# A block-sparse attention with two gated layers on one core: the second batch's value means, two iterations later

## The chip, the cores and the metric

The kernel runs on one core of one Trainium2 chip. The metric is the device time of one execution in microseconds (us). The core has five engines that take their instructions in order, each from its own stream: TensorE (PE in the profile, with its weight loads as PEld), VectorE (DVE), ScalarE (ACT), GpSimd (POOL) and SyncE (SP), which here only issues transfers.

## The reference

Three stages, all in float32. The attention has 2 batches, 8 heads, 768 positions and 64 values per head. Each query sees the keys within 15 positions of its own and, for the whole sequence, 24 block entries: the maximum of the keys and the mean of the values over blocks of 32.

```python
k_sum = k.reshape(B, H, nb, block, D).max(axis=3)
v_sum = v.reshape(B, H, nb, block, D).mean(axis=3)
scores_l = scale * np.matmul(q, k.transpose(0, 1, 3, 2))
mask_l = np.abs(pos[:, None] - pos[None, :]) < window
scores_s = scale * np.einsum('bhsd,bhnd->bhsn', q, k_sum) + np.log(block)
scores_all = np.concatenate([np.where(mask_l, scores_l, -1e9), scores_s], axis=-1)
a = softmax(scores_all)                  # written out, with 1e-09 on the sum
out = np.matmul(a, np.concatenate([v, v_sum], axis=2))
...
h = x @ w_in;  g = h / (1 + exp(-1.702 * h));  x = g @ w_out            # 512 -> 2048 -> 512
...
x = (sigmoid(x @ w_gate) * (x @ w_val)) @ w_out2                        # 512 -> 1536 -> 512
```

The 2 x 768 rows of the attention, with the 8 heads side by side, are the 1536 rows of the two gated layers.

## The kernel before

**Units.** The attention is cut into 24 units: 2 batches, 3 groups of 256 queries, 4 pairs of heads. Units 0 to 11 are the first batch, 12 to 23 the second. A unit's scores are 4 tiles of 128 x 128: 64 queries of two heads against 32 columns for the block entries and 96 for a window of keys. The loop runs over t from -1 to 26, and each iteration t issues the steps of several units, as `ORDER` (L789) says: `w_copy` (POOL, keys and block maxima of unit t+1 to the tile `kx`), `b_pe` (PE, scores `ps_s` of unit t), `b_max` (DVE, L715), `b_exp` (ACT, L723), `n_inv` and `n_mul` (DVE and POOL, unit t-1), and for unit t-3 `c_pe` (PE, transposes `ps_p`, L743), `c_copy` (L748, on ACT up to unit 9, on DVE from unit 10), `d_pe` (PE, products with the values, `ps_x`, L762), `d_hi` (ACT, L780) and `d_lo` (DVE, L783).

**Means of the values.** `sum_load` (L657) brings the transposed values of one pair of heads to a tile `vt`, of which there are two buffers, so the third load waits for the first sum and the fourth for the second. `sum_v` (L668) sums them over blocks of 32 on DVE (L672, into `vm`). `sum_lay` (L677) transposes the four pieces on PE (`ps_v`, L681, with an identity) and scales them on ACT into `vs` (L682). `put_v` (L648) copies `vs` to the first 32 rows of four places of the tile `vwin`, by a transfer; `load_v` (L640) brings the windows of the values to its other 96 rows (L646). `vwin` holds two groups of 256 queries in turn. The second batch's first group is read by `d_pe` of unit 12, in iteration 15. `ps_v` and `ps_x` share one PSUM tag, "x", with two buffers.

**Keys.** `load_k` (L624) brings the second batch's keys in iterations 8 to 11, one pair of heads in each; `prep_k` (L684) takes their block maxima on DVE (L688) at the start of iterations 10 to 13.

**Other work of the same stretch.** The first weights of the gated layers are loaded (`fetch`, L229) and split into two parts by `load` (L118; DVE L132, L150, L157, ACT L140, L155), called through `pull`. From iteration 10 on `filler` (L843) issues products of the first gated layer (`ps_h`, `ps_o`, L489; gate on ACT L522, DVE L500, ACT L508, POOL L509), so that PE has work beside the attention. After the attention PE does the gated layers.

**Order.** SP's transfers are issued in the order in which the program writes them, apart from a few weight pieces, and a transfer that waits holds those behind it. On PE, DVE, ACT and POOL a planner orders the instructions when the program is built: it takes what it expects to be ready, earlier program lines first, by its own costs. On the chip each engine keeps to that order. SP's order around the change, from iteration 7 on, is in each iteration: the query block of unit t+5, a transposed value (t = 7 to 10), the window values and `put_v` (t = 7, 11, 15, 19), the keys (t = 8 to 11), and weight pieces.

Of the kernel before, what the change touches and what calls it, by code (L numbers as in the profile page):

```python
# [29 lines left out]
def attention_moe_moe2_kernel(ctx: ExitStack, tc: tile.TileContext, ins: dict, out: bass.AP):  # L30
# [15 lines left out]
    NG = NQB // G  # L46
# [182 lines left out]
    def fetch():  # L229

        if pieces:
            name, src = pieces.pop(0)
            n, m = src.shape[1], src.shape[2]

            home, tag = (xp, "xH") if name == "1_0_1" else (wraw, "raw")
            raw = home.tile([P, n * m], U32, tag=tag, name=f"{tag}{name}")
            nc.sync.dma_start(out=raw.rearrange("p (a n) -> p a n", a=n), in_=src)
            raws.append((raw, (P, n, m // 2)))
# [355 lines left out]
    def pull(n):  # L594
        for _ in range(n):
            next(coming, None)
# [9 lines left out]
    with tc.manual_schedule(engines={mybir.EngineType.SP}), ExitStack() as es:  # L606
# [17 lines left out]
        def load_k(b, hp):  # L624

            t = kp.tile([P, SH], F32, tag="k", name=f"k{b}_{hp}")
            nc.sync.dma_start(out=t, in_=k[b, hp])
            kraw[b, hp] = t

        def load_q(u, eng):  # L630

            b, g, hp = units[u]
            t = qp.tile([P, G, P], F32, tag="q", name=f"q{u}")
            eng.dma_start(out=t.rearrange("p i c -> p (i c)"), in_=q[b, g, hp])
            qbd[u] = t
# [4 lines left out]
        def load_v(b, g):  # L640
            c = (b * NG + g) % 2 * G
            first_row = v[b, g * G * QB:g * G * QB + P - W0, :]
            src = bass.AP(
                first_row.tensor, first_row.offset, [first_row.ap[0], [QB * H * D, G], [1, H * D]]
            )
            nc.sync.dma_start(out=vwin[W0:P, c:c + G, :], in_=src)  # L646

        def put_v(b, g, eng=nc.sync):  # L648
            c = (b * NG + g) % 2 * G
            src = vsum[b][0:W0].unsqueeze(1).to_broadcast([W0, G, H * D])  # L650
            eng.dma_start(out=vwin[0:W0, c:c + G, :], in_=src)
# [5 lines left out]
        def sum_load(b, hp):  # L657
            if (b, hp) == (0, 2):
                early = xp.tile([P, 2, KC * TB // 2], F32, tag="xL", name="vt_early")
                vtl["early"] = [early[:, i, 0:S] for i in range(2)]  # L660
            if b == 0 and hp > 1:
                t = vtl["early"][hp - 2]
            else:
                t = vp.tile([P, S], F32, tag="vt", bufs=2, name=f"vt{b}_{hp}")
            nc.sync.dma_start(out=t, in_=vt[b, hp])
            vtl[b, hp] = t

        def sum_v(b, hp):  # L668
            if hp == 0:
                vpart[b] = vp.tile([P, HP, W0], F32, tag="vm", name=f"vm{b}")  # L670
                nc.vector.memset(vpart[b], 0.0)
            nc.vector.tensor_reduce(  # L672
                out=vpart[b][:, hp, 0:NB], in_=vtl.pop((b, hp)).rearrange("p (n t) -> p n t", t=BLK),
                axis=AX.X, op=ALU.add,
            )

        def sum_lay(b):  # L677
            r = vpart.pop(b)
            ps = ps_a.tile([W0, H * D], F32, tag="x", name="ps_v", bufs=2)
            for hp in range(HP):  # L680
                nc.tensor.matmul(ps[:, hp * P:(hp + 1) * P], lhsT=r[:, hp], rhs=ident, start=True, stop=True)  # L681
            nc.scalar.activation(vsum[b][0:W0], ps, AF.Copy, scale=1.0 / BLK)  # L682

        def prep_k(b, hp):  # L684
            ks = kp.tile([P, W0], F32, tag="ks", name=f"ks{b}_{hp}")
            nc.vector.memset(ks, 0.0)
            own = kraw[b, hp][:, HALO:HALO + S].rearrange("p (n t) -> p n t", t=BLK)
            nc.vector.tensor_reduce(out=ks[:, 0:NB], in_=own, axis=AX.X, op=ALU.max)  # L688
            kmax[b, hp] = ks
# [164 lines left out]
        for t in range(-1, NU + LD):  # L854
            now[0] = t

            u = t + 2
            if u < NU and units[u][1] == 0:
                prep_k(units[u][0], units[u][2])
            for part, lag in ORDER:  # L860
                if 0 <= t - lag < NU:
                    part(t - lag)
            if 0 <= t < NU - 5:
                load_q(t + 5, nc.sync)
            if t == -1:
                sum_v(0, 0)
                sum_v(0, 1)
            if t == 0:
                sum_v(0, 2)
                sum_v(0, 3)  # L870
                sum_lay(0)
                load_v(0, 1)
                put_v(0, 1, nc.scalar)
            if t in (2, 5, 8):
                fetch()
            if t in (7, 8, 9, 10):
                sum_load(1, t - 7)
            if t in (8, 9, 10, 11):
                sum_v(1, t - 8)
            if t == 11:  # L880
                sum_lay(1)

            if t % HP == HP - 1 and HP < t < NU - HP:
                c = t // HP + 1
                load_v(c // NG, c % NG)
                put_v(c // NG, c % NG)
            if 8 <= t < 8 + HP:
                load_k(1, t - 8)
            if t >= 1:
                pull(1 if t < 6 or t > 9 else 2)  # L890
            for _ in range(2 if t >= 8 else 1):
                next(fill, None)
# [168 lines left out]
```

## Time and profile before

| | us |
|---|---|
| median of 3 runs | 617.34 |
| lowest and highest run | 616.87, 618.29 |
| the profiled execution | 616.23 |
| its span in the profile | 614.4 |
| PE busy | 601.0 |
| DVE busy | 448.6 |
| ACT busy | 313.3 |
| POOL busy | 201.6 |

A group of the profile names a line of the kernel, an engine, an operation, and the tiles out<-in. Idle time of an engine counts only where it lies on the chain that ends last. A busy PE is not PE at its peak, since products are pipelined and their recorded spans overlap.

### The profile page before, as it was taken

The numbers are of one execution on the slowest core, as the hardware profiler recorded it, in microseconds if no ns is written. First come the engines' busy times: TensorE is split into PE (matmuls) and PEld (weight loads), VectorE is DVE, ScalarE is ACT, GpSimd is POOL, SyncE is SP. The second block draws the span as 40 slices with busy tenths as digits, with TensorE's granted clock in tenths as the row PEclk, the third lists the DMA queues.
The fourth block names the chain that finished last, engine by engine and source line by source line (L and its number), as shares of the span: only waits on it lengthen the run. The fifth ranks groups of instructions, "written<-read, shape, count | busy, mean of one in ns | idle before, by whom it ended". The sixth has DMA issues, their size and how long they took to land.

```text
span 614.4 us, 8772 instructions
## 1 busy us (share of the span) xinstructions
PE 601.0 (98%) x3348; PEld 500.4 (81%) x3348; DVE 448.6 (73%) x655; ACT 313.3 (51%) x620; POOL 201.6 (33%) x164
## 2 busy tenths in 40 slices
PE   7888999999999999999999999999999999999997
PEld 4766787788888888888888888898898898898896
DVE  6699665399929988877559889668759669777434
ACT  4678657566424645535345667635445246344230
POOL 6897685323331243413322021022022022122030
PEclk9899999999999999999999999999999999999999
DMA  9998753012402421321002023222222222200014
GB/s 314 343 313 298 233 138 70 2 69 69 137 1 68 138 68 69 103 104 65 5 1 69 0 69 103 104 69 69 69 69 69 68 69 70 68 2 1 0 51 155
DMA packets 25162, 58.10 MB, mean 95 GB/s; under 512 B 1569, under 2 KB 1825, under 8 KB 25121
## 3 DMA queue, kind: packets, MB, share of 16 engines
q1 hardware_dynamic: 24400, 56.24, 28.3%
q10 hardware_dynamic: 720, 1.31, 0.6%
q8 instruction: 26, 0.43, 0.3%
q14 instruction: 16, 0.12, 0.1%
HBM read 53.08 MB, written 3.15 MB: 92 GB/s over the span
## 4 chain that ended last, share of the span: by engine, by line
PE 92%; DVE 3%; POOL 1%; issue 1%; DMA 1%; ACT 1%; SPq 0%; ACTq 0%; POOLq 0%; DVEq 0%
PE ps_o L489 37%; PE ps_y L197 16%; PE ps_x L197 10%; PE ps_v L197 10%; PE ps_h L489 8%; PE ps_h L197 4%; PE ps_s L710 3%; PE ps_x L762 2%; PE ps_p L743 1%; DMA vt<-in_vt 1%; POOL kx L699 1%; DVE nm L715 1%; ACT e L723 1%; DVE da L150 1%; DVE vm L672 0%
## 5 line engine op out<-in xcount | busy, mean ns | idle before, releaser
L509 POOL TENSOR_TENSOR gl<-sg,gh 128x512 fp32r<-128x512 f32 x84 | 125.6, 1500 | 377.3 <-ACT gh L508 290.1
L575 DVE TENSOR_TENSOR acc<-ps_o,acc 128x512 f32<-128x512 f32 x143 | 96.5, 685 | 66.5 <-PE ps_o L489 66.3
L489 PE MATMUL ps_o<-gl,w_1H 128*128 128x512 f32 x192 | 75.3, 393 | 0.0
L489 PE MATMUL ps_o<-gh,w_1H 128*128 128x512 f32 x192 | 74.7, 390 | 0.0
L489 PE MATMUL ps_o<-gh,w_1L 128*128 128x512 f32 x192 | 71.9, 396 | 1.8 <-ACT gh L508 1.7
L508 ACT CAST gh<-sg 128x512 fp32r<-128x512 f32 x84 | 51.7, 622 | 31.1 <-DVE sg L500 24.7
L489 PE MATMUL ps_o<-w_2L,gh 128*128 128x512 f32 (+1 forms) x146 | 56.6, 388 | 0.0
L489 PE MATMUL ps_o<-w_2H,gh 128*128 128x512 f32 (+1 forms) x146 | 56.4, 386 | 0.0
L489 PE MATMUL ps_o<-w_2H,gl 128*128 128x512 f32 (+1 forms) x146 | 56.3, 389 | 0.1
L150 DVE SCALAR_TENSOR_TENSOR da<-da,db 128x1024 uint32<-128x1024 uint32 x34 | 47.7, 1404 | 9.7 <-ACT da L140 9.1
L140 ACT ACTIVATE da<-da 128x1024 f32<-128x1024 f32 x34 | 36.1, 1061 | 21.8 <-DVE da L132 21.8
L489 PEld LDWEIGHTS ps_o<-gh,w_1L 128*128 128x128 f32 x192 | 35.9, 188 | 9.6 <-ACT gh L508 2.2
L489 PEld LDWEIGHTS ps_o<-gl,w_1H 128*128 128x128 f32 x192 | 36.1, 188 | 7.3 <-POOL gl L509 0.2
L489 PEld LDWEIGHTS ps_o<-gh,w_1H 128*128 128x128 f32 x192 | 36.1, 188 | 7.3
L723 ACT ACTIVATE e<-ps_s,nm 128x128 f32<-128x128 f32 x96 | 34.2, 376 | 9.1 <-DVE nm L715 6.9
L699 POOL TENSOR_SCALAR kx<-k 128x384 f32<-128x384 f32 x24 | 32.2, 1344 | 15.7 <-PE ps_s L710 7.1
L489 PE MATMUL ps_h<-xH,w_0L 128*128 128x512 f32 x80 | 31.7, 407 | 0.8 <-DVE db L132 0.8
L710 PE MATMUL ps_s<-kx,q 128*128 128x128 f32 x192 | 30.5, 307 | 1.9 <-POOL kx L699 1.8
L489 PEld LDWEIGHTS ps_o<-w_2H,gh 128*128 128x128 f32 x146 | 27.4, 188 | 5.7
L710 PEld LDWEIGHTS ps_s<-kx,q 128*128 128x128 f32 x192 | 27.5, 215 | 5.6 <-POOL kx L699 3.3
L489 PEld LDWEIGHTS ps_o<-w_2L,gh 128*128 128x128 f32 x146 | 27.5, 188 | 5.0
L489 PEld LDWEIGHTS ps_o<-w_2H,gl 128*128 128x128 f32 x146 | 27.4, 188 | 5.2 <-DVE acc L575 0.3
(244 smaller groups left out, 1495.5 us busy)
## 6 DMA issues: line engine op xcount, KB each, us to landing
raw<-in_moe_w_out SPq DMA_DIRECT2D x13, 1024.0 KB, 4.9
raw<-in_moe_w_in SPq DMA_DIRECT2D x8, 1024.0 KB, 7.3
raw<-in_moe_w_gate SPq DMA_DIRECT2D x6, 1024.0 KB, 5.0
raw<-in_moe_w_val SPq DMA_DIRECT2D x6, 1024.0 KB, 5.1
q<-in_q SPq DMA_DIRECT2D x20, 256.0 KB, 8.9
vwin<-in_v SPq DMA_DIRECT2D x6, 768.0 KB, 9.4
k<-in_k SPq DMA_DIRECT2D x8, 400.0 KB, 7.2
out<-acc SPq DMA_DIRECT2D x11, 256.0 KB, 2.0
```

The source lines that it names most:

```text
L140: nc.scalar.activation(af, af, AF.Prelu, scale=REBIAS, alpha=-2.0 ** 32)
L150: ins = nc.vector.scalar_tensor_tensor(out=a, in0=a, scalar=3, in1=b, op0=ALU.logical_shift_left, op1=ALU.bitwise_or)
L197: nc.tensor.matmul(ps, lhsT=a[x][:, kk, :], rhs=b[y][:, kk, :], start=start and i == 0, stop=i == n - 1, skip_group_check=True,)
L489: nc.tensor.matmul(ps, lhsT=a, rhs=b, start=i == 0, stop=i == n - 1)
L508: nc.scalar.copy(gh, sg)
L509: nc.gpsimd.tensor_tensor(out=gl, in0=sg, in1=gh, op=ALU.subtract)
L575: added[layer, g, blk, m] = nc.vector.tensor_tensor(out=a[:, m, :], in0=ps, in1=a[:, m, :], op=ALU.add)
L699: nc.gpsimd.tensor_scalar(out=to, in0=x, scalar1=scale, scalar2=None, op0=ALU.mult)
L710: nc.tensor.matmul(ps[:, j, :], lhsT=t[:, j, :], rhs=kt[:, j, :], start=False, stop=j == G - 1)
L715: nc.vector.tensor_reduce(out=nm, in_=live["s", u], axis=AX.X, op=ALU.max, negate=True)
L723: nc.scalar.activation(e[:, j, :], s[:, j, :], AF.Exp, bias=nm[:, j:j + 1], accum_out=sm[:, j:j + 1])
L762: nc.tensor.matmul(ps[64 * e:64 * e + 64, j, :], lhsT=x[:, h * D:(h + 1) * D], rhs=y[:, j, 64 * e:64 * e + 64], start=n == 0, stop=n == le ...
```

## The change

The loads of the second batch's transposed values move from iterations 7 to 10 to iterations 9 to 12, the sums from 8 to 11 to 10 to 13, and `sum_lay` from 11 to 13. `put_v(1, 0)`, which copies the second batch's means to its first group's places, moves from iteration 11, where it followed `load_v(1, 0)`, to iteration 13 behind `sum_lay`; `load_v(1, 0)` stays in iteration 11. The later groups' `put_v` stay (NG is 3, and c counts the groups over both batches).

```diff
             if t in (2, 5, 8):
                 fetch()
-            if t in (7, 8, 9, 10):
-                sum_load(1, t - 7)
-            if t in (8, 9, 10, 11):
-                sum_v(1, t - 8)
-            if t == 11:
+            if t in (9, 10, 11, 12):
+                sum_load(1, t - 9)
+            if t in (10, 11, 12, 13):
+                sum_v(1, t - 10)
+            if t == 13:
                 sum_lay(1)
+                put_v(1, 0)
 
             if t % HP == HP - 1 and HP < t < NU - HP:
                 c = t // HP + 1
                 load_v(c // NG, c % NG)
-                put_v(c // NG, c % NG)
+                if c != NG:
+                    put_v(c // NG, c % NG)
             if 8 <= t < 8 + HP:
                 load_k(1, t - 8)
```

## Rows read from the trace of the kernel before

**Rows 1.** The page: busy time, share of the span, instructions.

```profile
PE 601.0 (98%) x3348; PEld 500.4 (81%) x3348; DVE 448.6 (73%) x655; ACT 313.3 (51%) x620; POOL 201.6 (33%) x164
```

**Rows 2.** Windows: stretch, its length, busy us by engine, clock, DMA share, GB/s.

```profile
40.00:60.00 20.00, 17.93 (x155) 13.80 (x155) 19.32 (x33) 17.39 (x50) 15.79 (x14) 1.00 0.99 321
60.00:80.00 20.00, 19.29 (x138) 15.49 (x138) 13.14 (x26) 13.76 (x40) 14.54 (x15) 1.00 0.68 220
80.00:100.00 20.00, 20.00 (x170) 16.15 (x169) 12.19 (x28) 11.17 (x43) 13.24 (x16) 1.00 0.51 120
```

**Rows 3.** The chain that ended last, from 46 us: start, us, engine, tile, line.

```profile
46.21 0.69 DVE nm L715
...
57.75 1.56 DVE w_1L L157
...
62.87 0.69 DVE pt L748
...
63.69 0.69 PE ps_x L762 x16
...
69.07 5.46 PE ps_h L489 x24
```

**Rows 4.** Timeline of DVE, 40 to 70 us: start, us, instruction, [idle before <-releaser].

```profile
40.35 0.92 DVE L672 TENSOR_REDUCE vm<-vt 128x24 f32<-128x768 f32 x1
...
48.55 0.95 DVE L672 TENSOR_REDUCE vm<-vt 128x24 f32<-128x768 f32 x1
...
57.08 0.68 DVE L748 COPY pt<-ps_p 128x512 f32<-128x512 f32 x1
...
60.48 0.94 DVE L672 TENSOR_REDUCE vm<-vt 128x24 f32<-128x768 f32 x1
...
68.76 0.95 DVE L688 TENSOR_REDUCE ks<-k 128x24 f32<-128x768 f32 x1 [2.57 <-DMA k<-in_k]
```

**Rows 5.** Timeline of SP, 31 to 64 us: start and us of each issue.

```profile
31.38 0.38 SPq L665 DMA_DIRECT2D vt<-in_vt  x1
...
41.29 0.33 SPq L665 DMA_DIRECT2D vt<-in_vt  x1
...
50.89 0.38 SPq L646 DMA_DIRECT2D vwin<-in_v  x1
62.60 0.61 SPq L651 DMA_DIRECT2D vwin<-vs  x1
63.30 0.54 SPq L627 DMA_DIRECT2D k<-in_k  x1
```

**Rows 6.** Waits of SP (whole span) and of PEld (40 to 80 us).

```profile
SPq L651 <- ACT vs L682: 11.2, 1, 11.2
PEld ps_x L762 <- DVE xL L783: 0.6, 2, 0.4
```

**Rows 7.** Tile vt: durations, landing; transfers of means issued at 62.60 and 32.69.

```profile
L672 DVE TENSOR_REDUCE vm<-vt x6: 917/945/954, 8.0 to 60.5; 128x24 f32<-128x768 f32 x6
...
DMA to landing us min/median/max: 5.9/7.4/12.2
...
vwin<-vs SPq DMA_DIRECT2D x1, 256.0 KB, 3.3
...
vwin<-vs SPq DMA_DIRECT2D x1, 256.0 KB, 11.4
```

**Rows 8.** Timeline of PE, 51 to 75 us.

```profile
51.84 0.62 PE L681 MATMUL ps_v<-ident,vm 128*32 128x128 f32 x4
...
60.92 0.69 PE L762 MATMUL ps_x<-pt,vwin 128*64 128x64 f32 x16
...
74.46 0.45 PE L762 MATMUL ps_x<-pt,vwin 128*64 128x64 f32 x6
```

**Rows 9.** Timeline of POOL: copies of keys at 58 and 79 us.

```profile
58.36 2.22 POOL L699 TENSOR_SCALAR kx<-k 128x384 f32<-128x384 f32 x1
...
79.38 1.17 POOL L699 TENSOR_SCALAR kx<-k 128x384 f32<-128x384 f32 x1
```

## The prediction

> **What bounds the kernel now.** I read the page first: TensorE (PE) is busy 601.0 of 614.4 us [rows 1], so all that PE does not stand idle for is fixed work, and the change alters none of it. The reader should next look where PE does stand idle. The windows answer that: from 40 to 60 us PE is busy 17.93 of 20, from 60 to 80 it is 19.29, and from 80 on it is full [rows 2]. In the same 40 to 60 VectorE (DVE) is busy 19.32 and ScalarE (ACT) 17.39. So the attention stage is set by the vector side, and the rest by PE. The change acts at about 31 to 75 us, on the seam between the two.
>
> The chain of waits says where the seam lies. From 46.21 on it runs through DVE alone (maximum of unit 11, weight splits, block sums), up to the copy of unit 11's transposes at 62.87, which ends at 63.56; at 63.69 it enters PE with unit 11's value products and stays there, with long runs of products such as the 24 at 69.07 [rows 3]. What comes earlier or later at 63.69 comes earlier or later at the end, as PE has a backlog from there on. A loss after it counts only if PE runs dry.
>
> The timeline of DVE shows the first of the four block sums at 40.35, the second at 48.55 and the last at 60.48, each 0.92 to 0.95 long, and at 68.76 the block maximum of the fourth keys after an idle 2.57 that a transfer of keys ended [rows 4]. The timeline of SP shows why that transfer was late: the four transposed values go out from 31.38 on (the third at 41.29), the values of the next window at 50.89, and then the copy of the means waits until 62.60; the keys follow at 63.30 [rows 5]. SP's own waits put 11.2 us on that copy, for ACT's means [rows 6].
>
> **The change, part by part.**
>
> *Loads and sums moved by two iterations.* Four loads, four sums and a memset stay as many; nothing is added. Of the sums the first (40.35) stands before the DVE chain begins, the other three inside it, ahead of the copy at 62.87. After the change the first load goes out where the third does now (about 41), the second about 45, the third beside the row at 50.89, and the fourth about 56, since its buffer waits for the second sum. With 7.4 us to landing, the median of these loads [rows 7], the sums can start at about 48, 53, 58 and 64. The first and second are inside the chain, the fourth is behind it, the third lands at the edge. Three sums inside the chain become two or three. I take two: one sum of 0.95 us leaves the chain. Bounds: 0 (three remain) and 1.9 (only one remains before 62.87, if the sums really move by two whole units). What the sums that leave do next is covered: behind 63.69 DVE has the idle 2.57 at 66 [rows 4], and PE has the runs from 69.07 [rows 3]; without that backlog each would cost its 0.95 there.
>
> *The products that transpose the sums.* These sixteen products share a ring of two PSUM buffers with the value products of the units. Now they take a buffer at 51.84 and hold it until ACT reads the means, just ahead of 62.60; the value products of unit 10 start at 60.92, when the vector engine has emptied the only other buffer [rows 8]. The waits put 0.6 us in two places on that emptying [rows 6]. After the change the buffer is asked for two units later, so units 9 and 10 have both. I credit the recorded 0.6 us. Bounds: 0 (the engine's order holds them anyway) and 3.2, if unit 10 could start right behind the copy of its transposes (57.08 and 0.68 [rows 4]) rather than at 60.92; of this PE had other products to do for much of the time, so I stay by the recorded wait. Holding the buffer later falls under the backlog of PE.
>
> *The transfer of the means.* One transfer of 256 KB with the same 0.6 us of issue on SP, moved from iteration 11 to 13. What stands behind it on SP changes: today the fourth keys, query blocks and two weight pieces stand behind it; afterwards the keys and most of the query blocks go ahead, the weight pieces still stand behind. The keys then go out at about 51 instead of 63.30, and the idle 2.57 of DVE goes. I price this at nothing: PE was covered there by the runs at 69.07. There is a cost: the keys' block maximum (0.95) may now be ready before the copy at 62.87 and be put ahead of it. I take nothing for it and 0.95 as its bound, which would eat the first term. The window's values stay in iteration 11, with no new wait ahead of them.
>
> *The new wait.* Unit 12's value products are the first that read the moved means. They start at 74.46 now [rows 8], and the means have about 9 us of slack, as their transfer took 3.3 us in an empty queue; among other traffic the same transfer took 11.4 [rows 7]. From the start of the last sum to the issue is 2.1 us today (60.48 to 62.60). So in the new order: fourth sum at 64, issue at 66, landing at 69.5 by the quick row and 77.5 by the slow one, against unit 12 at about 73. The queue should be nearly empty by then, since what stood behind has gone ahead, so I take the quick row, and no cost; bound 4.5.
>
> *The sum.* 0.95 + 0.6 = 1.55 us off the profiled execution's 616.23 gives 614.7. That execution lies 1.1 below the median of the runs, 617.34; on the median the forecast is 615.8.
>
> **A rule against it.** The rows show GpSimd's copy of keys taking 2.22 us at 58.36 [rows 9], beside a weight split on DVE at 57.75 that took 1.56 [rows 3], and 1.17 at 79.38; the sums themselves keep to 917 to 954 ns [rows 7]. So a sum may be a pause in which GpSimd runs free, and a chain with fewer sums has its weight splits closer together; two more stretched copies would cost 2 x 1.05 us on the way to the scores. This is rival 3 below. The Trainium skill, SBUF — State Buffer, Who interferes with whom, says that a DVE instruction with two SBUF inputs contends with a GpSimd instruction that reads SBUF, and that a tensor_reduce never does on trn2; by that rule the stretched copies are blocked ones and the sums are harmless, so swapping sums for splits can only hurt GpSimd. The stretched row agrees in direction; no row here shows the lock itself.
>
> **The rivals.**
>
> 1. *Nothing to measure.* Three sums stay inside the chain, or the fourth keys' maximum takes the place of the one that left; only some of the 0.6 remains. For it: the loads land 7 to 12 us after their issue, so a shift by two iterations need not be two units on DVE, and the planner orders DVE by readiness. Against it: the last sum can hardly land before 63. Time: 617.34 less 0 to 0.6, about 617.1.
>
> 2. *The means come too late (slower).* Place: PE at unit 12's value products. It decides if the transfer is issued after 73 - 3.3 = 69.7, or if it lands at the slow row's pace. For it: the moved sums ran about two units behind their own iteration (the sum of iteration 11 stands at unit 13), and the same lag from iteration 13 puts the last one beside unit 15, at the same point as the products that need it; the fourth load can't go out before the second sum; a load took up to 12.2 us [rows 7], which alone puts the issue at 70 or later. Against it: DVE has room after 65, and the DMA queue too. Price: landing at 77.5 instead of 73 is 4.5, less about 0.5 of other units' products and the 1.55 won: 617.34 + 2.5 = 619.8.
>
> 3. *GpSimd loses what DVE wins.* The 2.1 us of two stretched copies against 0.95 won: 618.5.
>
> 4. *DVE stands still for a late load.* DVE executes in order, and a sum placed for 7.4 us to landing that lands after 12.2 holds everything behind it, at worst inside the chain. In the trace all four sums were met without such a wait, against it; that the queue is full there speaks for it. Price: 4.8 us, less 1 to 2 of margin and the 1.55 won: 619.1.
>
> **How the numbers follow.** The forecast has 0.42, rival 1 0.26, rival 2 0.18, rival 3 0.06, rival 4 0.08. A difference of 0.2% is 1.23 us, about what a measurement can tell here. Forecast: faster, 0.42. Rivals 1 and 3 lie within 0.2%: 0.32. Rivals 2 and 4 are slower: 0.26. The range reaches down to 617.34 less the 1.9 of the first bound and half of the 3.2 of the second, 613.8, and up to 619.2, which takes in rivals 1, 3, most of 4 and the light half of 2; some 0.04 lies below and 0.13 above. The likeliest case alone spans 613.8 to 616.1.
>
> **What would show it.** Right: the fourth sum starts after the copy of unit 11's transposes, that copy ends at about 62.6 instead of 63.56, unit 11's value products start near 62, the transposing products start after unit 10's value products, the keys' transfer goes out near 51 with no idle 2.57 behind it, and from there PE is full as before. SP's wait for the means is still there, some 8 us long, in iteration 13. Wrong: a PE wait on the transfer of means ahead of unit 12's value products (rival 2), GpSimd copies of over 2 us in other places (rival 3), a DVE wait on a transposed value between 46 and 64 (rival 4), or unit 11's value products still at 63.7 (rival 1). The whole forecast falls if PE shows new idle time anywhere behind 64, as the planner may order the four engines anew from iteration 7 on.

## The result, and the profile after

The changed kernel took 621.37 us (median of 4 runs, 620.82 to 622.0), the kernel before 617.27 on the same chip (4 runs): a ratio of 1.0074, with a 95% interval of 1.0061 to 1.0086. It is 0.7% slower, where the forecast was 615.8 us and faster; 621.37 lies above the range too. The profiled execution has a span of 619.7 us against 614.4, 5.3 us more, and that is what has to be found.

The page after, as in [rows 1]:

```profile
PE 600.8 (97%) x3348; PEld 499.6 (81%) x3348; DVE 449.0 (72%) x655; ACT 316.0 (51%) x622; POOL 201.2 (32%) x164
```

PE has the same work. ACT has two instructions more and 2.7 us more of work: a pair of table loads of 1.28 each. So PE stands idle longer, or runs at a lower clock. The windows after answer to [rows 2] (same columns), with finer ones behind:

```profile
40.00:60.00 20.00, 16.93 (x157) 13.04 (x158) 18.36 (x34) 17.04 (x50) 13.32 (x13) 0.95 1.04 339
60.00:80.00 20.00, 20.00 (x129) 15.34 (x128) 13.00 (x22) 11.86 (x31) 14.88 (x14) 0.96 0.31 94
80.00:100.00 20.00, 18.71 (x155) 14.99 (x154) 13.37 (x28) 11.00 (x48) 14.14 (x16) 1.00 0.91 249
100.00:120.00 20.00, 17.81 (x150) 14.18 (x150) 8.91 (x23) 16.43 (x48) 8.37 (x8) 1.00 0.00 1
...
55.00:58.00 3.00, 0.79 (x8) 0.62 (x7) 3.00 (x8) 2.97 (x11) 2.20 (x2) 1.00 1.05 253
58.00:60.00 2.00, 1.90 (x19) 1.27 (x19) 2.00 (x6) 2.00 (x5) 0.50 (x2) 0.53 1.06 235
60.00:62.00 2.00, 2.00 (x10) 1.27 (x8) 2.00 (x2) 1.97 (x10) 2.00 (x2) 0.62 1.03 318
62.00:64.00 2.00, 2.00 (x10) 1.41 (x9) 2.00 (x5) 0.00 (x0) 2.00 (x3) 1.00 0.53 196
```

And four windows of the kernel before that are not in [rows 2]:

```profile
55.00:58.00 3.00, 1.31 (x18) 1.13 (x13) 3.00 (x6) 2.98 (x5) 2.74 (x4) 1.00 1.06 258
...
60.00:62.00 2.00, 1.91 (x22) 1.10 (x22) 2.00 (x5) 0.55 (x3) 1.83 (x2) 1.00 0.04 16
62.00:64.00 2.00, 1.39 (x14) 0.89 (x16) 2.00 (x5) 2.00 (x11) 0.53 (x1) 1.00 0.06 15
100.00:120.00 20.00, 19.99 (x166) 15.52 (x166) 9.93 (x24) 14.26 (x48) 9.08 (x10) 1.00 0.01 2
```

Multiply PE's busy time by the granted clock (PEclk, a share of the full 2.4 GHz) and the loss can be placed. The reader is to see three episodes:

- **40 to 64 us.** Before: 17.93 [rows 2] + 1.91 + 1.39 = 21.23 us of work. After: 16.93 less 0.47 x 1.90 for the clock of 0.53, plus 0.62 x 2.00, plus 2.00 = 19.28. Lost: 1.95.
- **80 to 100.** Before full [rows 2]; after 18.71. Lost: 1.29.
- **100 to 120.** 19.99 before, 17.81 after. Lost: 2.18.

Together 5.42, close to the 5.3 of the span. From 64 to 80 both are full. Up to 40 us the same count gives 31.2 before and 30.9 after, so the balance is good to some 0.4 us.

What PE waits for in the three is in its timeline after (start, us, products, idle time and its releaser):

```profile
58.10 0.59 PE L708 MATMUL ps_s<-mask,pick 128*128 128x512 bf16 x1 [2.31 <-ACT e L723]
58.62 1.12 PE L762 MATMUL ps_x<-pt,vwin 128*64 128x64 f32 x16
...
60.44 1.20 PE L489 MATMUL ps_o<-gh,w_1L 128*128 128x512 f32 x2
...
73.05 0.41 PE L681 MATMUL ps_v<-ident,vm 128*32 128x128 f32 x2
...
79.02 0.69 PE L762 MATMUL ps_x<-pt,vwin 128*64 128x64 f32 x16
...
86.66 0.69 PE L762 MATMUL ps_x<-pt,vwin 128*64 128x64 f32 x16 [0.74 <-DVE pt L748]
...
88.70 0.50 PE L489 MATMUL ps_o<-gh,w_1L 128*128 128x512 f32 x1 [0.55 <-DVE acc L575]
...
106.37 0.50 PE L489 MATMUL ps_o<-gh,w_1L 128*128 128x512 f32 x1 [0.58 <-DVE sg L500]
...
112.44 0.69 PE L762 MATMUL ps_x<-pt,vwin 128*64 128x64 f32 x16 [1.62 <-DVE pt L748]
```

*First.* At 58.10 the mask product of unit 15 (it puts the mask into the unit's scores; the other products of those scores come only at 73.38) waits 2.31 us for the PSUM buffer that the exponentials of unit 12 empty, and holds all behind it. ACT's timeline, before and then after, tells why those are late and what else is. A gate batch is two tiles `sg` of the first gated layer that pass the sigmoid together; `gh` is ACT's copy of such a tile, which the products `ps_o` read.

```profile
52.78 1.28 ACT L522 ACT_TABLE_LOAD   x1
...
56.24 0.64 ACT L508 CAST gh<-sg 128x512 fp32r<-128x512 f32 x1
56.90 1.28 ACT L723 ACT_TABLE_LOAD   x1
...
59.58 0.63 ACT L508 CAST gh<-sg 128x512 fp32r<-128x512 f32 x1
```

```profile
52.85 1.28 ACT L522 ACT_TABLE_LOAD   x1
54.15 1.08 ACT L522 ACTIVATE sg<-ps_h 128x512 f32<-128x512 f32 x2
55.25 1.28 ACT L723 ACT_TABLE_LOAD   x1
56.54 0.37 ACT L723 ACTIVATE e<-ps_s,nm 128x128 f32<-128x128 f32 x1
...
59.13 1.16 ACT L508 CAST gh<-sg 128x512 fp32r<-128x512 f32 x2
...
103.70 1.28 ACT L522 ACT_TABLE_LOAD   x1
107.26 1.28 ACT L723 ACT_TABLE_LOAD   x1
```

Before, the gate batch's first copy `gh` comes at 56.24, ahead of the exponentials, and the second at 59.58, behind them; after, the exponentials with their table load come first and both copies at 59.13. So the products `ps_o` that need `gh` start at 60.44. Before, they started at 56.94:

```profile
56.94 0.50 PE L489 MATMUL ps_o<-gh,w_1L 128*128 128x512 f32 x1 [1.69 <-ACT gh L508]
```

And behind the wait PE's clock falls to 0.53 and 0.62 in the profiled execution, that is, it spends most of 58 to 62 us at 1.2 GHz.

*Second.* The chain of waits after runs through the moved means:

```profile
73.20 1.28 ACT L522
74.49 0.60 ACT sg L522
75.09 0.48 ACT vs L682
75.58 0.61 SPq L651
...
76.24 5.75 DMA raw<-in_moe_w_out
...
82.01 1.77 DVE db L132
```

SP issues a weight piece right behind the means, DVE stands 1.75 us idle for it, and PE gets the lateness at 86.66 and 88.70: 0.74 and 0.55 us, together the 1.29.

*Third.* The table loads at 103.70 and 107.26 are the extra pair; ACT is busy 16.43 of 20 us instead of 14.26, and PE waits 0.58 at 106.37 and 1.62 at 112.44, both on the chain of waits that runs through these loads.

DVE's timeline answers to [rows 4]:

```profile
51.19 0.94 DVE L672 TENSOR_REDUCE vm<-vt 128x24 f32<-128x768 f32 x1
...
53.40 0.68 DVE L715 TENSOR_REDUCE nm<-ps_s 128x4 f32<-128x512 f32 x1
...
57.93 0.94 DVE L672 TENSOR_REDUCE vm<-vt 128x24 f32<-128x768 f32 x1
...
62.13 0.68 DVE L748 COPY pt<-ps_p 128x512 f32<-128x512 f32 x1
...
63.06 0.94 DVE L672 TENSOR_REDUCE vm<-vt 128x24 f32<-128x768 f32 x1
...
64.86 0.94 DVE L688 TENSOR_REDUCE ks<-k 128x24 f32<-128x768 f32 x1
...
66.56 0.92 DVE L672 TENSOR_REDUCE vm<-vt 128x24 f32<-128x768 f32 x1
```

### The profile page after: what moved, and what is told of

It is laid out like the page before. It is cut to its first block, busy times and chain, and to the rows that moved or that the text cites. A ratio compares the mean times of both kernels' runs of the same rounds, so it can differ in the third digit from the quotient of the medians.

```text
span 619.7 us, 8778 instructions
## 1 busy us (share of the span) xinstructions
PE 600.8 (97%) x3348; PEld 499.6 (81%) x3348; DVE 449.0 (72%) x655; ACT 316.0 (51%) x622; POOL 201.2 (32%) x164
## 2 busy tenths in 40 slices
DMA packets 25161, 58.10 MB, mean 94 GB/s; under 512 B 1568, under 2 KB 1824, under 8 KB 25120
## 3 DMA queue, kind: packets, MB, share of 16 engines
q1 hardware_dynamic: 24400, 56.24, 28.3%
q10 hardware_dynamic: 720, 1.31, 0.6%
## 4 chain that ended last, share of the span: by engine, by line
PE 85%; DMA 8%; ACT 3%; DVE 3%; issue 0%; SPq 0%; ACTq 0%; DVEq 0%
PE ps_o L489 36%; PE ps_y L197 15%; PE ps_x L197 10%; PE ps_v L197 10%; PE ps_h L489 7%; PE ps_h L197 4%; DMA raw<-in_moe_w_out 3%; DMA xH<-in_moe_w_out 2%; DMA vt_early<-in_vt 2%; PE ps_x L762 1%; DMA q<-in_q 1%; ACT e L723 1%; PE ps_p L743 1%; ACT L723 1%; ACT L522 1%; DVE db L132 1%
## 5 line engine op out<-in xcount | busy, mean ns | idle before, releaser
L132 DVE TENSOR_SCALAR db<-raw 128x1024 uint32<-128x1024 uint32 x33 | 31.6, 959 | 3.6 <-DMA raw<-in_moe_w_out 3.2
L710 PE MATMUL ps_s<-kx,q 128*128 128x128 f32 x192 | 28.6, 296 | 3.8 <-POOL kx L699 2.3
L710 PEld LDWEIGHTS ps_s<-kx,q 128*128 128x128 f32 x192 | 26.0, 206 | 7.6 <-POOL kx L699 3.7
```

What stands on the lines that cost most here:

```text
L132: ins = nc.vector.tensor_scalar(**x)
L710: nc.tensor.matmul(ps[:, j, :], lhsT=t[:, j, :], rhs=kt[:, j, :], start=False, stop=j == G - 1)
```

## The experiments

**Theory 1, the order.** The moved work costs little. The planner, given other due work, writes other orders for PE and ACT, and in a few places these make PE wait. **Theory 2, the moved work itself.** Sums and means are late, and what needs them pays. In the kernels, `behind(a, b)` has the planner place instruction a behind instruction b. It adds no work, but the rest of the plan follows from it, so more than this pair can move. The diffs are shortened: `ins` and `live[...]` name instructions, the lines that store them are left out, and remarks behind # are added. Ratios are to the kernel before on the same chip; the runs come from several chips, so compare ratios rather than times.

| run | median us | ratio, 95% |
|---|---|---|
| after | 621.37 | 1.0074 (1.0061 to 1.0086) |
| e4_mask15 | 621.84 | 1.0079 (1.0059 to 1.0099) |
| e7_lay_first | 621.9 | 1.009 (1.0071 to 1.0109) |
| e2_act_queue | 620.5 | 1.0066 (1.0051 to 1.0081) |
| e5_one_table_pair | 619.12 | 1.0042 (1.0027 to 1.0057) |
| e9_gh_first | 617.05 | 1.001 (1.0 to 1.0021) |
| e13_gh_act | 617.93 | 1.0013 (1.0002 to 1.0024) |
| e3_one_later | 620.03 | 1.005 (1.0033 to 1.0068) |
| e12_one_later_gh | 617.44 | 1.0013 (1.0004 to 1.0022) |
| e1_means_late | 619.4 | 1.0058 (1.0039 to 1.0076) |
| e14_means_late_table | 616.12 | 0.999 (0.9981 to 0.9999) |
| e11_before_exp_first | 619.09 | 1.0045 (1.003 to 1.006) |
| e15_before_gh | 616.9 | 0.9999 (0.999 to 1.0008) |

**e4_mask15: the waiting mask product moved out of the way.** After, with one order more:

```diff
-            nc.tensor.matmul(ps, lhsT=pick, rhs=mask[:, g:g + G, :], start=True, stop=False)
+            ins = nc.tensor.matmul(ps, lhsT=pick, rhs=mask[:, g:g + G, :], start=True, stop=False)
+            u == 15 and behind(ins, live["d10"])     # d10: value products of unit 10
```

> The changed kernel with one order on PE altered: the mask product of unit 15 (one product of 0.4 us, needed only at 73) goes behind the value products and transposes of unit 10 instead of ahead of them; nothing else moves on any engine. In the changed trace PE stands idle 2.31 us ahead of that product at 58.10, and then shows a granted clock of 0.53 and 0.62 up to 62. Theory 1 (order: the loss is made of a few places where a planner's new order makes PE wait): 1.5 to 3 us off the changed kernel's 621.4, about 619. Theory 2 (late means: the loss comes from the transfer of the means at 75.58, which holds SP and pushes unit 12): nothing, 621 to 621.8, as the means come no earlier.

621.84 us: nothing won. PE's timeline shows the wait moved on:

```profile
57.20 0.69 PE L762 MATMUL ps_x<-pt,vwin 128*64 128x64 f32 x16 [1.51 <-DVE pt L748]
...
60.31 1.22 PE L489 MATMUL ps_o<-gh,w_1L 128*128 128x512 f32 x2 [1.35 <-ACT gh L508]
```

Unit 10's value products start earlier (57.20), and then PE stands for `gh`. The mask product was only the first in the line; what PE lacked next was ACT's `gh`.

**e7_lay_first: the means earlier.** After, with the last products that transpose the sums ahead of the second gate batch's products:

```diff
+                (g, blk, f) == (1, 0, 0) and held_up.append(live["lay", 1])
                 held.append(project(w[0], w[1], f, blk, "ps_h"))   # its first product: behind(ins, held_up.pop())
```

> The changed kernel with one order on PE altered: the last transposing product of the sums goes ahead of the 24 products of the second gate batch rather than behind 12 of them. The sum ends at 67.5, so ACT's means should come at about 70.5 and their transfer at 71 instead of 75.58, unit 12's value products at about 74.5 instead of 79.02, and what stands behind on SP 4.5 us earlier. Theory 2: most of the 4.1 us comes back, 617.5 to 619. Theory 1: only the part near 85 to 90 us, where DVE waits 1.75 for a weight piece that stood behind the means on SP: 619.5 to 621.

621.9 us: nothing won, though SP issued the means 3.85 us earlier than the 75.58 of after:

```profile
71.73 0.61 SPq L651 DMA_DIRECT2D vwin<-vs  x1
```

PE does 9.00 us of work from 80 to 90, where after does 8.71. Theory 2, as far as the lateness of the means goes, falls.

**e2_act_queue: the means past SP's queue.**

```diff
-                put_v(1, 0)
+                put_v(1, 0, nc.scalar)
```

> The changed kernel with the transfer of the means issued from ACT's queue, directly behind the scaling that it waits for, rather than from SP's; the means come no earlier, but the weight pieces and query blocks behind it on SP go out from 60 on. Theory 2 in the form that SP's held queue is what costs: DVE's wait of 1.75 at 82 and what follows on PE (1.3 us of idle between 86 and 89) goes, 619.5 to 620. In the form that unit 12 is late: nothing, 621 to 621.8, plus up to 0.7 us of issue time on ACT. Theory 1: the same 621 to 621.8, or 620 if the place near 85 hangs on that weight piece.

620.5 us. The second episode shrinks as it should: the weight piece goes out at 59.64, DVE does not wait for it from 76 to 88, and PE does 9.80 us of work from 80 to 90 where after does 8.71. Of that 1.1 us the timed ratio shows at most a part; the two intervals overlap, so the size is open.

**e5_one_table_pair: the extra pair of table loads out.** After, with the exponentials of unit 20 behind the second sigmoid of the third gate batch:

```diff
+            (g, blk) == (0, 1) and behind(live["exp20", 0], live["sg"])
```

> The changed kernel with one order on ACT altered: the exponentials of unit 20 go behind the second sigmoid of the third gate batch, so that ACT loads its tables once there and back instead of twice (two loads of 1.28 us fewer, near 103 to 108 us). Theory 1: the 1.62 us for which PE waits at 112.44, behind an ACT chain with those loads, goes wholly or mostly: 619.4 to 620.2. Theory 2: at most 0.3 us, 621.1.

619.12 us, 0.32% or 2.0 us less than after by the ratios, for a third episode of 2.18. From 100 to 120 PE does 19.97 us. The first episode stays (an idle 2.90 at 58.37).

**e9_gh_first: both copies `gh` ahead of unit 12's exponentials.** The kernel before has only the first of them ahead, so the expectation below is not exact where it says "as they stand in the kernel before".

```diff
+                u == 12 and j == 0 and behind(ins, live["gh", (1, 0, 0, 1)])   # ins: first exponential of unit 12
```

> After's kernel, with the exponentials of unit 12 placed behind the copies of the two activated tiles of the first gate batch, as they stand in the kernel before; the rest of the plan follows from that, and it too has one pair of table loads fewer behind 100 us. Theory 1 (order: after's ScalarE puts unit 12's exponentials with two table loads ahead of those copies, so TensorE waits for them at 58 to 60 us and its clock falls): the first products of the gate batch's second half start at about 57 us instead of 60.4, the granted clock stays at 1.00 from 50 to 64 us, and with the saved table pair the time is 617.0 to 618.5 us. Theory 2 (the moved work itself costs: sums and means are late): both are where after has them, and no more than the table pair's 2 us is won: 619.0 to 619.6.

617.05 us: the whole loss is gone but 0.1%, with the move in place. The sums start at 50.80, 58.03, 61.87 and 65.26, 1.3 us earlier than in the changed kernel at most. The means do leave 3.84 us earlier, but in e7 they left as early as that and nothing was won. PE's timeline, ACT's and SP's:

```profile
57.53 0.73 PE L489 MATMUL ps_o<-gh,w_1L 128*128 128x512 f32 x2 [1.79 <-ACT gh L508]
```

```profile
56.84 1.16 ACT L508 CAST gh<-sg 128x512 fp32r<-128x512 f32 x2
58.02 1.28 ACT L723 ACT_TABLE_LOAD   x1
```

```profile
71.74 0.61 SPq L651 DMA_DIRECT2D vwin<-vs  x1
```

The clock is 1.00 in every window from 50 to 64; PE does 21.31 us of work from 40 to 64, 10.00 from 80 to 90 and 19.54 from 100 to 120. One order at 55 us put all three right but for the 0.45 from 100 to 120: the plan that follows from it has no further table pair, and the weight piece, issued at 72.41 instead of 76.24, no longer makes DVE wait. By the ratios about 4 us are recovered (0.64%), of which e5 measured 2.0 for the pair; the rest, by difference, belongs to the first gate batch and what follows from it.

**e11_before_exp_first: that order put into the kernel before.** Nothing of the change is in it:

```diff
+                u == 12 and j == 3 and behind(live["gh", (1, 0, 0, 0)], ins)   # ins: last exponential of unit 12
```

> The kernel before, nothing of the change in it, with the copy of the first activated tile of the first gate batch placed behind the exponentials of unit 12, which is after's order on ScalarE; it also gets more table loads. Theory 1 (order): it loses as after does without moving a sum or a transfer, a wait of TensorE and a lower granted clock between 55 and 65 us: 619 to 621 us. Theory 2 (the moved work itself costs): ScalarE has room, 617 us, no more than 0.2% over before.

619.09 us, 0.45% slower with nothing moved. But not by the way I expected: the clock stays 1.00 from 40 us on. PE waits 1.04 at 61.35 and loses 0.51 us from 40 to 64; 0.31 is lost from 80 to 90, and 1.90 from 100 to 120, where the extra table pair appears:

```profile
103.03 1.28 ACT L522 ACT_TABLE_LOAD   x1
106.59 1.28 ACT L723 ACT_TABLE_LOAD   x1
```

So one early order decides a table pair 45 us later, and that is most of the 2.4 us by which the medians differ. (The profiled execution, at 620.48 the slowest of the four, lost a further 1.6 us ahead of 40 us, where its clock was 0.94 and 0.89, well ahead of the edited place.)

**e1_means_late: loads, sums and products in place, only the transfer moved.**

```diff
-            if t in (9, 10, 11, 12):
-                sum_load(1, t - 9)
+            if t in (7, 8, 9, 10):
+                sum_load(1, t - 7)
...
+            if t == 11:
+                sum_lay(1)
             if t == 13:
-                sum_lay(1)
                 put_v(1, 0)
```

> After with its loads, sums and transposing products back where before has them (iterations 7 to 11); the transfer of the means alone stays two iterations late. Theory 1 (order): sums and first gate batch as before, so no wait at 58 to 60 us and no lower clock there; a further pair of table loads late in the run, as in after: 616.5 to 619 us. Theory 2 (late means): the means still leave at iteration 13, so most of the loss stays: 619.5 to 621.5 us.

619.4 us. My premise that the means leave late was wrong: SP issued the transfer at 62.98 (62.60 in before [rows 5]), as soon as ACT had scaled the means (62.36, 0.59 long), as what now stands ahead of it on SP was gone by then. Yet the time is 0.58% over. The clock is 1.00 up to 64, and PE does 21.10 us of work up to there; the loss is from 100 to 120, where PE does 17.96, behind an extra pair of table loads at 100.94 and 104.23, and 0.66 more at 121.68:

```profile
103.39 0.73 PE L489 MATMUL ps_o<-gh,w_1L 128*128 128x512 f32 x2 [1.77 <-ACT gh L508]
```

**e14_means_late_table: the same without that pair**, by the edit of e5.

> The version that moves the transfer of the means alone (619.4 us; its transfer left at 62.98 us, hardly later than before's 62.60, but it has one pair of table loads more than before at 101 to 105 us, with a wait of TensorE of 1.77 us), now with the exponentials of unit 20 behind the second sigmoid of the third gate batch, which takes that pair out. Theory 1 (order): 616.5 to 617.3 us, as before. Rival (something else in the moved transfer costs): over 618.5 us.

616.12 us, level with before, and the 0.66 at 121.68 is gone too. The order that brings the pair was the loss.

**e3_one_later: all of it by one iteration instead of two** (loads in 8 to 11, sums in 9 to 12, the rest in 12).

> The same change by one iteration instead of two: loads, sums, transposing products and transfer of the means. Theory 1 (order): the time hangs on the order that the planner finds, not on the distance; anything from 615.5 to 622 us, and where its profile shows no wait of TensorE with a lower clock at 50 to 65 us and no further table pair, 616 to 617.5. Theory 2 (the cost grows with the distance): about half of after's loss, 618.5 to 620 us.

620.03 us. It is at the edge of theory 2's number, and theory 1's range takes in nearly everything, so the time alone tells the two apart no better than that. But its profile has the first episode worse than after (17.95 us of work from 40 to 64, counted as above), none of the third (20.00), and a clock of 0.70 and 0.50 from 60 to 64:

```profile
58.76 0.38 PE L708 MATMUL ps_s<-mask,pick 128*128 128x512 bf16 x1 [1.99 <-ACT e L723]
60.21 0.73 PE L489 MATMUL ps_o<-gh,w_1L 128*128 128x512 f32 x2 [1.08 <-ACT gh L508]
```

**e12_one_later_gh: e3 with the order of e9.**

> The change by one iteration instead of two, with the exponentials of unit 12 held behind the two copies of the first gate batch's activated tiles, as in the run that took after's loss away. The run by one iteration without this took 620.0 us, with 2.0 and 1.1 us of TensorE waits for those exponentials and copies and a clock of 0.70 and 0.50 behind them. Theory 1 (order): those waits go and the time is 616 to 617.5 us. Theory 2 (the moved work itself costs): 619 us or more.

617.44 us: 1.005 becomes 1.0013. So by one iteration as by two, the order is the loss. (Its profile has a lower clock elsewhere, 0.58 and 0.57 from 50 to 58, behind a wait of 1.91 for a copy of keys; that execution was the slowest of its 11, 618.54.)

**e13_gh_act: e9 with the means on ACT's queue.**

> After with unit 12's exponentials behind those copies (617.05 us), and the transfer of the means issued on ScalarE's queue instead of SP's; TensorE's order is the same in both. Theory 1 (what is left of the loss is the weight pieces that SP holds behind the means, 1.1 to 1.4 us in after): the pieces start before the means and the time is 615.8 to 616.8 us, at or below before. Rival (TensorE's backlog covers the late pieces in this order): 617.0 as without it.

617.93 us, no better than e9: the rival is right. With the first order mended, PE is full from 80 to 90 in e9 anyway; issuing the weight piece at 61.00 instead of 72.41 wins nothing more.

**e15_before_gh: the order of e9 in the kernel before.**

> The kernel before with unit 12's exponentials behind both copies of the first gate batch's activated tiles (before has them between the two copies), nothing moved. It tells whether this order by itself is worth something: if the version of after with it stands level with before only because the order wins and the move loses, this is 615 us or less; if the move is worth nothing either way, it is 616.3 to 617.3 us.

616.9 us, ratio 0.9999: the order brings before nothing. So e9 is not a gain of the order that hides a loss of the move; what the move does by itself is no gain, and a loss of about 0.1%, which e9, e12 and e13 have left over (their intervals reach to 0.24%).

## Why the prediction was wrong

**The bound and the seam: right.** PE's work did not change, and all of the 5.3 us is PE standing idle or at the lower clock. The prediction did not price the clock, which in the profiled execution took 1.65 us of them. And I looked for the effect at one place, the copy at 62.87, and for losses only behind 64. The first loss was the wait that ended at 58.10.

**One sum leaves the chain: right, and worth nothing.** Loads went out at 37.74, 44.12, 52.16 and 58.89; sums started at 51.19, 57.93, 63.06 and 66.56, 2.6 to 5.1 us later than forecast. Two stood ahead of the copy of unit 11's transposes, as I took, and it started at 62.13 instead of 62.87: 0.74 of the 0.95. But unit 11's value products came at 65.75, not at 62: PE had other products ahead of them in its order.

**The PSUM buffer: right, under-sized, and worth nothing.** Unit 10's value products started at 58.62 instead of 60.92, 2.3 us earlier, near the bound of 3.2 and not the 0.6 taken. PE did them in place of the `ps_o` products that it lacked, so nothing was won.

**The keys: right.** Issued at 53.05 (forecast 51), block maximum at 64.86 behind the copy, no idle 2.57.

**The new wait: the issue was wrong, the harm too.** I carried over "from start of last sum to issue is 2.1 us". It was 9.0 (66.56 to 75.58): the last transposing product stood behind 12 products of the second gate batch (done at 73.05), and ACT put a table load and a sigmoid ahead of the scaling. By rival 2's own point, 69.7, the means were too late. But unit 12's value products were ordered later too, at 79.02, and PE did not wait for them. What the late transfer did hold up was a weight piece behind it on SP. I had seen that the weight pieces "still stand behind" and gave that no price; the chain through it is where 1.29 us of the span went, and e9 shows that under another order it goes.

**The step that failed** is the sum. It took 1.55 us off and left the order of everything else as it was: the planner's new order stood in it at nothing, without a reason, and it measured some 4 us (1.0074 less 1.001). My last sentence named "the planner may order the four engines anew", but gave it neither a chance nor a price. It needed both: DVE's maximum for unit 12 came at 53.40 instead of 55.88, and its exponentials followed the sigmoids directly, ahead of `gh`. That the moved sums brought on this order is an argument from the two timelines; why the planner chose it is open. That the order is the cost is shown: putting it right takes 1.0074 to 1.001 with the move in place, and 1.005 to 1.0013 with the smaller move; putting it into the kernel before costs 0.45%, by its profile most of it through the table pair that it brings on.

**The rivals.** Rival 1, nothing to measure, gives nearly the number of the move with the orders mended (1.001 by two iterations, 1.0013 by one), but not its reason: only two sums stayed ahead of the copy, and the fourth keys' maximum came behind it. Rival 2's wait of PE for the means did not occur. Rival 3 is wrong in sign: GpSimd's copies of keys from 46 to 64 us took up to 1.55 us, where [rows 9] has 2.22. Rival 4 did not occur; from 46 to 64 us DVE never stood for a transposed value.

The Trainium skill, ScalarE: Activation LUTs, Table sets: the hidden batching unit, says to do all calls of one table set before those of the other. The pair taken out in e5 and e14 agrees, at about 2 us in e5. The first episode is of another kind: the number of loads there is the same in before and after, two of 1.28 us, and the loss comes from which work stands behind the second.

None of the kernels run here beats the kernel before by more than 0.1%.

## What to carry to other kernels

Where a planner writes the order, a moved line can be an edit to every engine's order, and here its price was that order's, not that of the work moved: compare the orders first, then look for the places where an engine that was full stands idle. Multiply the bound engine's busy time by its granted clock, window by window, against the kernel before; the differences should add up to about that of the spans (here 5.42 of 5.3), and each then leads to a wait or two. And test a loss by putting the old order back with the move in place, before blaming the move.

## What was not expected of the hardware

A wait of 2.31 us in a stretch that was already thin (PE busy 0.79 of 3.00 us from 55 to 58) was followed by a clock of 0.53 and 0.62 over 4 us, at a cost of 0.47 x 1.90 + 0.38 x 2.00 = 1.65 us, some seven tenths of the wait. The same stretch in the kernel before, busy 1.31 of 3.00, kept 1.00. e11 kept 1.00 as well, with 2.18 of 3.00, 1.40 of 2.00 and 0.82 of 2.00 in the windows from 55 to 62. What decides between them was not tried, and the order alone does not: these are one execution of each kernel, and the mean clock of a kernel's executions differs. Of the four of the changed kernel the profiled one has 0.997 (621.5 us) and the fastest 1.000; at 620.82 us that one is still 3.55 over the median of before, so most of the loss stands without the lower clock. In e3 the clock seems to weigh more: one execution at 1.000 took 617.69 us, the other four, at 0.991 to 0.996, took 619.9 to 620.88.
